# Unit spacing, four accumulator banks at the end, earlier value copies and a split last tile in an attention + feed-forward kernel

## Chip, cores, metric

The kernel runs on one core of a Trainium2 chip. The metric is device time in microseconds (us).

The engines: PE is TensorE (matmuls), PEld its weight loads, DVE VectorE, ACT ScalarE, POOL GpSimd, SP SyncE.

## Reference

```python
# q, k, v: (8 batches, 8 heads, 576, 64); bias_table: (32, 8)
scores = q @ k.T / 8 + bias(bucket(|i - j|), head)
x = softmax(scores) @ v            # as (4608 tokens, 512)
out = ((x @ w_a) * (x @ w_b)) @ w_out      # w_a, w_b: (512, 1536), w_out: (1536, 512)
```

Inputs and output are float32, and the kernel computes with bfloat16 operands.

## The kernel before

Attention goes through 32 slots, one for each batch and pair of heads. A slot makes scores on PE (`qk`), their exponentials on ACT (`ex`, 128x1024 each), scales these by a bias factor on DVE (`mul`), and multiplies the previous slot's weights by the values (`av`). The feed-forward network of a finished batch fills PE in between, as *units*. A unit is four 512-column matmuls into one PSUM bank: `pa` (emptied by ACT into `ha`), `pb` (emptied by DVE, multiplied by `ha`, into `g`), or a third of an output tile `po`. There are 9 chunks of 512 tokens, 36 units each (the first chunk has 44, some of them half as wide). The last two chunks run after attention has ended.

```python
# PSUM, 8 banks: scores 2 x 2 banks, av 1, transposes 1, feed-forward 2
ps_sc = pool(bufs=2); ps_av = pool(bufs=1); ps_tr = pool(bufs=1); ps_ff = pool(bufs=2)
wrk = pool(bufs=2)                 # SBUF: ha, output tiles ob, reciprocals: two of each
# ... cut ...
def ff_b(c, df, lo=0, n=512):
    pb = ps_ff.tile([128, 512], FP32, tag="ffn")
    for mc in range(4):
        nc.tensor.matmul(out=pb[:, 0:n], lhsT=wb_sb[df // 4][:, mc, ...], rhs=xn_sb[mc][...], ...)
    nc.vector.tensor_tensor(out=g_sb[df][...], in0=pb[...], in1=ff["ha"][...], op=MULT)
# ... cut: ff_a is the same with w_a, and an ACT copy to ha ...
def ff_o(c, tt, part):             # token tile tt, a third of 12 matmuls
    ...
    if part == 2:
        ob = wrk.tile([128, DM], FP32, tag="ob")
        nc.scalar.activation(out=ob, in_=po, func=Copy)
        # last chunk: two stores of 64 rows, both issued by ACT
        for hh in range(2):
            nc.scalar.dma_start(out=out[r0:r0 + ST, :], in_=ob[64 * hh:64 * hh + 64, :])
# ... cut ...
# one slot s; U puts a unit, A(...) are the previous slot's values
steps = [(qk(s, 0), ex(s, 0)),
         U, ex(s, 1), A(0, 1, 2), U, mul(s, 0), t_q(s + 1), U,
         mul(s, 1), A(3, 4), (qk(s, 2), ex(s, 2)), U,
         ex(s, 3), t_k(s + 1), U, t_x(s - 1), mul(s, 2), U, mul(s, 3), U,
         (qk_tail(s), ex_tail(s)), U, U, mul_tail(s)]
# ... at the end of every slot:
v_next(s)                          # even slots: DVE copies the values of four heads into vm
```

Between the second score pair `qk(s, 2)` and `qk_tail` stand four units in a row with nothing else on PE.

The softmax here doesn't subtract the row's maximum and nothing guards it: scores larger than these inputs give would overflow.

## Time and profile before

Three runs: 431.69 us median (430.83 to 432.91).

| read from the trace of before | value |
|---|---|
| PE busy | 412.0 of 430.5 us |
| spacing of 512-column matmuls | 0.216 us |
| a pair pa + pb, last two chunks | 1.875 us (eight matmuls: 1.72) |
| a DVE product `g` from a bank | 0.69 us |
| value copy on DVE | 0.42 us |
| ACT copy of 128x512 from PSUM | 0.60 us |

From the page of the kernel before come the busy times (us, share of the span, instructions; one line) and the chain that ended last:

```profile
PE 412.0 (96%) x3406; PEld 210.3 (49%) x3459; DVE 238.0 (55%) x560; ACT 248.1 (58%) x346; POOL 130.0 (30%) x187
...
PE 88%; DVE 7%; issue 2%; ACT 1%; DVEq 0%; ACTq 0%
```

PE sets the time. But 96% busy does not mean 4% of holes. A matmul's record lasts 0.38 us while the next can start 0.216 us after it, so records overlap and cover small holes. Holes are read from the starts. A few matmul records are missing, and a gap of exactly one more matmul (0.216 us) is such a record.

The timeline of before in the last chunk (start, duration, engine, line, what; in brackets idle time and what ended it):

```profile
397.15 0.38 PE L492 MATMUL pa_2_0_5469<-xn_134,wa_124 128*128 128x512 bf16 x1
...
397.51 0.38 PE L502 MATMUL pb_2_0_5476<-xn_131,wb_127 128*128 128x512 bf16 x1
...
398.65 0.69 DVE L505 TENSOR_TENSOR g_137<-pb_2_0_5476,ha_2_0_5474 128x512 bf16<-128x512 f32 x1 [1.18 <-PE pb_2_0_5476 L502]
...
399.02 0.38 PE L492 MATMUL pa_3_0_5482<-xn_134,wa_124 128*128 128x512 bf16 x1
...
399.39 0.38 PE L502 MATMUL pb_3_0_5489<-xn_131,wb_127 128*128 128x512 bf16 x1
```

The last matmul of pa starts at 397.15 and the first of pb at 397.51: 0.36 us instead of 0.216. At 398.65 DVE begins to empty that pb's bank and ends at 399.34. The next pb starts at 399.39, while the matmul before it started at 399.02. Every pair loses 0.15 us to a bank that is not yet empty.

The timeline of before, PE only, in slot 17, after its second score pair:

```profile
185.08 0.38 PE L330 MATMUL qk_3_2905<-QB_116,KB_118 64*128 64x512 bf16 x2
185.39 0.39 PE L502 MATMUL pb_1_0_2910<-xn_131,wb_127 128*128 128x512 bf16 x1
...
186.26 0.38 PE L492 MATMUL pa_2_0_2918<-xn_131,wa_124 128*128 128x512 bf16 x1
...
186.91 0.38 PE L492 MATMUL pa_2_0_2918<-xn_134,wa_124 128*128 128x512 bf16 x1
187.28 0.38 PE L502 MATMUL pb_2_0_2928<-xn_131,wb_127 128*128 128x512 bf16 x1
...
189.00 0.22 PE L384 MATMUL qkt_2942<-ZB_120,KB_118 128*128 128x128 bf16 x1
```

From 186.91 to 187.28 is 0.37 us: the same hole. It opens at the third unit of the row, the pb at 187.28: DVE's product from the row's first bank, pb(1), ran from 186.53 to 187.22 (the same timeline, DVE only):

```profile
186.53 0.69 DVE L505 TENSOR_TENSOR g_136<-pb_1_0_2910,ha_1_0_2875 128x512 bf16<-128x512 f32 x1 [0.31 <-PE pb_1_0_2910 L502]
```

The timeline of before at the start of slot 19, with the value copy:

```profile
203.89 0.42 DVE L318 COPY vm_101<-vn_97 128x1024 bf16<-128x1024 bf16 x1
204.01 0.22 PE L448 MATMUL av_0_3153<-vt_103,att_113 128*128 128x130 bf16 x1
...
204.36 0.19 PE L452 MATMUL av_0_3153<-vm_101,at_0_2976 128*128 128x65 bf16 x1
```

The value matmul that reads `vm` (line 452) starts 0.35 us after the one ahead of it, just when the copy (203.89 to 204.31) has ended.

The timeline of before at the end (ACTq is ACT's sequencer issuing two stores):

```profile
423.22 0.60 ACT L516 ACTIVATE ob_2_5646<-po_2_5633 128x512 f32<-128x512 f32 x1 [1.99 <-PE po_2_5633 L512]
...
423.85 1.12 ACTq L523 DMA_DIRECT2D out_dram<-ob_2_5646  x2
...
425.39 0.38 PE L512 MATMUL po_3_5650<-wo,g_146 128*128 128x512 bf16 x1
425.81 0.60 ACT L516 ACTIVATE ob_3_5663<-po_3_5650 128x512 f32<-128x512 f32 x1 [1.99 <-PE po_3_5650 L512]
426.44 1.12 ACTq L523 DMA_DIRECT2D out_dram<-ob_3_5663  x2
```

### The profile page before, as it was taken

How to read it: one execution, taken by the hardware profiler on the slowest of the kernel's cores; microseconds unless marked ns; L12 is line 12 of the kernel's file. 1: busy time of each engine (PE TensorE's matmuls, PEld its weight loads, DVE VectorE, ACT ScalarE, POOL GpSimd, SP SyncE). 2: the span in 40 equal slices, each digit the busy share in tenths (PEclk: the TensorE clock that was granted, in tenths of full speed). 3: DMA queues.
4: the chain of work that ended last, by engine and by line, in shares of the span. 5: the costliest groups of instructions: out<-in, count | busy, mean ns of one | idle time of the engine just before them, and what ended most of it. 6: DMA issues, size and time to landing. Idle time of an engine off the chain costs nothing.

```text
span 430.5 us, 8709 instructions
## 1 busy us (share of the span) xinstructions
PE 412.0 (96%) x3406; PEld 210.3 (49%) x3459; DVE 238.0 (55%) x560; ACT 248.1 (58%) x346; POOL 130.0 (30%) x187
## 2 busy tenths in 40 slices
PE   8689899999999999999999999999999999999995
PEld 3366545455455545554555545544555454344442
DVE  5789667566654665466646664666546642321320
ACT  4676676676656666676566665676566642323221
POOL 9655458694009500870069004200000000000000
PEclk9789999999999999999999999999999999999999
DMA  8999999999149924995399919960420011002004
GB/s 110 195 202 186 205 138 186 163 175 152 23 88 162 160 36 87 132 146 77 63 118 145 120 24 123 123 88 14 109 56 15 15 40 73 1 24 75 0 2 98
DMA packets 139596, 42.46 MB, mean 99 GB/s; under 512 B 115962, under 2 KB 134938, under 8 KB 139554
## 3 DMA queue, kind: packets, MB, share of 16 engines
q0 software_dynamic: 81264, 18.89, 55.2%
q1 hardware_dynamic: 52850, 13.54, 21.7%
q10 hardware_dynamic: 5440, 9.47, 7.1%
q8 instruction: 27, 0.44, 0.5%
q14 instruction: 15, 0.12, 0.1%
HBM read 39.18 MB, written 9.45 MB: 113 GB/s over the span
## 4 chain that ended last, share of the span: by engine, by line
PE 88%; DVE 7%; issue 2%; ACT 1%; DVEq 0%; ACTq 0%
PE warm L207 1%; DVE g_143 L505 1%; PE trb L268 1%; DVE att_113 L419 1%; PE po_2_4609 L512 1%; PE po_2_3999 L512 1%; PE po_2_3376 L512 1%; PE po_2_2753 L512 1%; PE po_2_2130 L512 1%; PE po_1_2670 L512 1%; PE po_1_3916 L512 1%; PE po_3_5650 L512 1%; PE po_0_5379 L512 1%; PE po_0_5084 L512 1%; PE po_0_3878 L512 1%
## 5 line engine op out<-in xcount | busy, mean ns | idle before, releaser
L492 PEld LDWEIGHTS <-wa_124 128*128 128x128 bf16 x160 | 14.7, 98 | 17.8 <-issue 3.9
L502 PEld LDWEIGHTS <-wb_128 128*128 128x128 bf16 x144 | 13.3, 97 | 20.3 <-issue 7.1
L159 POOL DMA_DIRECT2D vt_104<-in_v_dram x8 | 4.9, 626 | 58.9 <-PE av_3_2722 L452 27.7
L502 PEld LDWEIGHTS <-wb_129 128*128 128x128 bf16 x144 | 12.9, 97 | 18.8 <-issue 7.0
L502 PEld LDWEIGHTS <-wb_127 128*128 128x128 bf16 x160 | 14.1, 97 | 16.2 <-issue 5.9
L159 POOL DMA_DIRECT2D vt_103<-in_v_dram x8 | 5.1, 645 | 55.5 <-PE av_3_3345 L452 27.4
L492 PEld LDWEIGHTS <-wa_125 128*128 128x128 bf16 x144 | 12.9, 98 | 16.5 <-issue 2.9
L492 PEld LDWEIGHTS <-wa_126 128*128 128x128 bf16 x144 | 12.9, 98 | 16.2 <-issue 2.8
L130 POOL DMA_DIRECT2D qn_93<-in_q_dram x24 | 18.3, 818 | 6.9 <-DMA wo<-in_moe_w_out_dram 6.1
L139 POOL DMA_DIRECT2D kn_95<-in_k_dram x24 | 18.2, 801 | 5.0 <-PE pb_3_256_951 L502 2.7
L130 POOL DMA_DIRECT2D qn_94<-in_q_dram x24 | 18.2, 807 | 2.2 <-DMA vn_97<-in_v_dram 1.9
L139 POOL DMA_DIRECT2D kn_96<-in_k_dram x24 | 18.1, 795 | 0.2 <-PE pb_11_0_1307 L502 0.2
L419 DVE TENSOR_TENSOR att_113<-att_113,W_88 128x512 bf16<-128x512 bf16 x8 | 3.4, 426 | 14.2 <-ACT att_113 L409 14.2
L448 PEld LDWEIGHTS <-att_114 128*128 128x128 bf16 x76 | 7.5, 99 | 3.9 <-DVE XG_123 L462 0.7
L408 ACT ACTIVATE att_114<-trb 128x64 bf16<-128x64 f32 x14 | 3.1, 224 | 10.8 <-PE trb L392 10.8
L408 ACT ACTIVATE att_113<-trb 128x64 bf16<-128x64 f32 x14 | 3.1, 224 | 10.7 <-PE trb L392 10.7
L448 PEld LDWEIGHTS <-att_113 128*128 128x128 bf16 x76 | 7.4, 98 | 3.6 <-DVE att_113 L421 0.2
L419 DVE TENSOR_TENSOR att_114<-att_114,W_91 128x512 bf16<-128x512 bf16 x8 | 3.4, 427 | 7.6 <-ACT att_114 L409 7.6
L505 DVE TENSOR_TENSOR g_135<-pb_0_0_5450,ha_0_0_5448 128x512 bf16<-128x512 f32 x1 | 0.7, 693 | 11.4 <-PE pb_0_0_5450 L502 11.4
L512 PEld LDWEIGHTS <-g_135 128*128 128x128 bf16 x36 | 3.5, 97 | 7.0 <-issue 4.5
L207 PE MATMUL warm<-zero_sb 128*128 128x512 bf16 x11 | 5.2, 581 | 1.5 <-DVE zero_sb L199 1.2
L121 POOL DMA_DIRECT2D vn_97<-in_v_dram x8 | 6.6, 828 | 0.0
(2743 smaller groups left out, 1515.9 us busy)
## 6 DMA issues: line engine op xcount, KB each, us to landing
vn_97<-in_v_dram POOLq DMA_DIRECT2D x8, 256.0 KB, 6.3
vn_98<-in_v_dram POOLq DMA_DIRECT2D x8, 256.0 KB, 7.0
wo<-in_moe_w_out_dram POOLq DMA_DIRECT2D x1, 1536.0 KB, 16.2
kn_95<-in_k_dram POOLq DMA_DIRECT2D x24, 64.0 KB, 5.2
qn_93<-in_q_dram POOLq DMA_DIRECT2D x24, 64.0 KB, 4.7
kn_96<-in_k_dram POOLq DMA_DIRECT2D x24, 64.0 KB, 4.9
qn_94<-in_q_dram POOLq DMA_DIRECT2D x24, 64.0 KB, 4.0
qn_93<-in_q_dram POOLq DMA_DIRECT2D x4, 128.0 KB, 4.2
```

The source lines that it names most:

```text
L121: nc.gpsimd.dma_start(out=dst[:, 256 * h0:256 * h1].rearrange("p (h x) -> p h x", x=256), in_=src[b, h0:h1, 0:SM, :].rearrange("h (p t) d ...
L130: nc.gpsimd.dma_start(out=by_tile(qn[b % 2])[:, h0 // 4, t, :, :], in_=q[b, h0:h1, 128 * t:128 * t + 128, :].transpose([1, 0, 2]))
L139: nc.gpsimd.dma_start(out=by_tile(kn[b % 2])[:, h0 // 4, t, :, :], in_=k[b, h0:h1, t:SM:NM, :].transpose([1, 0, 2]))
L159: nc.gpsimd.dma_start(out=vt[b % 2][64 * hh:64 * hh + 64, :, hh, 0:Dh], in_=v[b, hh:H:2, SM:S, :].transpose([1, 0, 2]))
L207: nc.tensor.matmul(out=warm[:, :], lhsT=zero_sb[:, 0:128], rhs=zero_sb[:, :], start=True, stop=True)
L408: nc.scalar.activation(out=at[:, m:m + ST], in_=pt, func=ACTF.Exp, scale=scale)
L419: nc.vector.tensor_tensor(out=x, in0=x, in1=e, op=MULT)
L448: nc.tensor.matmul(out=pav[:, slot, :, :], lhsT=weights_tail(p, jq), rhs=vt[i][:, hp, :, :], start=True, stop=True)
L492: nc.tensor.matmul(out=pa[:, 0:n], lhsT=wa_sb[df // 4][:, mc, 128 * (df % 4):128 * (df % 4) + 128], rhs=xn_sb[mc][:, 512 * c + lo:512 * c ...
L502: nc.tensor.matmul(out=pb[:, 0:n], lhsT=wb_sb[df // 4][:, mc, 128 * (df % 4):128 * (df % 4) + 128], rhs=xn_sb[mc][:, 512 * c + lo:512 * c ...
L505: nc.vector.tensor_tensor(out=g_sb[df][:, lo:lo + n], in0=pb[:, 0:n], in1=ff["ha"][:, 0:n], op=MULT)
L512: nc.tensor.matmul(out=po[:, :], lhsT=g_sb[df][:, 128 * tt:128 * tt + 128], rhs=wo_sb[:, df, :], start=(df == 0), stop=(df == NDF - 1))
```

## The change

Four ideas: (1) never more than two units in a row, with the late values or scores in between; (2) in the last two chunks, when no scores are made any more, units take turns on four banks, two of them from the score pool; (3) the value copy is made in mid-slot, a whole half slot before it is needed; (4) the last token tile is made in two column halves, each copied by ACT and DVE together and stored by SP and ACT in parallel.

```diff
+    def ff_bank(name):
+        ff["n"] += 1
+        if ff["late"] and ff["n"] % 4 >= 2:
+            return ps_sc.tile([128, 2, 512], FP32, tag="sc", name=name)[:, 0, :]
+        return ps_ff.tile([128, 512], FP32, tag="ffn", name=name)
 # pa, pb and po come from ff_bank (cut)
+    def ff_o_last(c, tt, half):
+        cs = slice(256 * half, 256 * half + 256)
+        po = ff_bank(f"po{c}_{tt}_{half}")
+        for df in range(NDF):
+            nc.tensor.matmul(out=po[:, 0:256], lhsT=g_sb[df][:, 128 * tt:128 * tt + 128],
+                             rhs=wo_sb[:, df, cs], start=(df == 0), stop=(df == NDF - 1))
+        ob = wrk.tile([128, DM], FP32, tag="ob", name=f"ob{c}_{tt}_{half}")
+        nc.scalar.activation(out=ob[:, 0:128], in_=po[:, 0:128], func=ACTF.Copy)
+        nc.vector.tensor_copy(out=ob[:, 128:256], in_=po[:, 128:256])
+        for hh, eng in enumerate((nc.sync, nc.scalar)):
+            r0 = S * (2 * tt + hh) + SM
+            eng.dma_start(out=out[r0:r0 + ST, cs], in_=ob[64 * hh:64 * hh + 64, 0:256])
 # ... cut ...
-            steps += [U, lambda: ex(s, 1), A(0, 1, 2), U, lambda: mul(s, 0), lambda: t_q(s + 1), U,
-                      lambda: mul(s, 1), A(3, 4), lambda: (qk(s, 2), ex(s, 2)), U,
-                      lambda: ex(s, 3), lambda: t_k(s + 1, ACT), U, lambda: t_x(s - 1),
-                      lambda: mul(s, 2), U, lambda: mul(s, 3), U,
-                      lambda: (qk_tail(s), ex_tail(s)), U, U, lambda: mul_tail(s)]
+            head = [U, lambda: ex(s, 1), A(0, 1, 2), U, lambda: mul(s, 0), lambda: t_q(s + 1), U,
+                    lambda: mul(s, 1)]
+            late = [A(3, 4), U, lambda: t_x(s - 1)]
+            pair = [lambda: v_next(s), lambda: (qk(s, 2), ex(s, 2)), U, lambda: ex(s, 3),
+                    lambda: t_k(s + 1, ACT), U, lambda: mul(s, 2)]
+            tail = [lambda: (qk_tail(s), ex_tail(s)), U, U, lambda: mul_tail(s)]
+            if s % 4 == 0:
+                steps += head + late + [U] + pair + [lambda: mul(s, 3)] + tail
+            else:
+                steps += head + pair + late + [lambda: mul(s, 3), U] + tail
         else:
+            ff["late"] = True
 # ... cut ...
-        if new:
+        if s == 4:
             v_next(s)
```

More of the change, by code (lines that the diff above doesn't have):

```diff
@@ L484, in t_x @@
             copy(eng, xn_sb[hp][:, c0:c0 + ST], ps[:, SM - q0:S - q0])
-    ff = {}
+    ff = {"late": False, "n": 0}
+    def ff_bank(name):
[3 more added lines that the diff above has]
+        return ps_ff.tile([128, 512], FP32, tag="ffn", name=name)
     def ff_a(c, df, lo=0, n=512):
-        pa = ps_ff.tile([128, 512], FP32, tag="ffn", name=f"pa{c}_{df}_{lo}")
+        pa = ff_bank(f"pa{c}_{df}_{lo}")
         for mc in range(NMC):
@@ L499, in ff_b @@
     def ff_b(c, df, lo=0, n=512):
-        pb = ps_ff.tile([128, 512], FP32, tag="ffn", name=f"pb{c}_{df}_{lo}")
+        pb = ff_bank(f"pb{c}_{df}_{lo}")
         for mc in range(NMC):
@@ L505, in ff_b @@
         nc.vector.tensor_tensor(out=g_sb[df][:, lo:lo + n], in0=pb[:, 0:n], in1=ff["ha"][:, 0:n], op=MULT)
+    def ff_o_last(c, tt, half):
[10 more added lines that the diff above has]
+            eng.dma_start(out=out[r0:r0 + ST, cs], in_=ob[64 * hh:64 * hh + 64, 0:256])
     def ff_o(c, tt, part):
         if part == 0:
-            ff["po"] = ps_ff.tile([128, 512], FP32, tag="ffn", name=f"po{c}_{tt}")
+            ff["po"] = ff_bank(f"po{c}_{tt}")
         po = ff["po"]
@@ L536 @@
         for tt in range(4):
+            if c == NCH - 1 and tt == 3:
+                units += [lambda c=c, tt=tt, half=half: ff_o_last(c, tt, half) for half in range(2)]
+                continue
             for part in range(3):
```

## The prediction

> **What bounds it.** TensorE. The page has PE busy 412.0 of 430.5 us (96%), DVE 55%, ACT 58%; the chain of waits is 88% PE. Busy hides waiting here, because a matmul record (0.38 us) is longer than the spacing of matmuls. So I read the spacing of starts in the timeline: 512-column matmuls start every 0.216 us (the Trainium skill, "TensorE: Matmul & The Clock Gate", Back-to-back issue gap, gives N/2.4 + 2.5 ns, also 216: the trace agrees), a feed-forward unit of 4 takes 0.86 us, a pair 1.72 us. Gaps of exactly one matmul are missing records. Granted clock is 1.00 after 30 us. The diff removes no matmul work; only holes in this stream can be saved.
>
> **Holes it aims at:**
>
> 1. Last two chunks (360 to 418 us): only two feed-forward banks. A pair takes 1.875 us, as at 397.51, 399.39, 401.26: pb starts right after DVE has emptied the preceding pb (0.69 us, starting 0.4 us after its matmuls). 22 holes of 0.15 us, 3.3 us in all. With four banks in rotation (two from the idle score pool) DVE (0.69 per 1.72 us) and ACT (0.60) keep up. Saved: 3.1 us.
> 2. Same hole from 75 to 346 us: four units stand in a row after the second score pair. 18 holes of 0.153 us, 2.75 us. With at most two in a row, 0.5 us or more of other matmuls lies in between, so a bank has 1.36 us to drain instead of 0.86; some 1.1 are needed. Working the order through with traced durations, exponentials (1.02 us) and scalings (0.68) leave only 0.1 us of slack in slots where DVE also has the value copy. Saved: 2.3 us.
> 3. Value copies (0.42 us on DVE) end a slot; the next slot's first value matmul waits for them: 0.30 us at 113.5, 158.8, 204.0, 249.3 and 340.1 us, 0.65 at 294.5. The one at 49.8 us (0.42) stays, since slot 4 keeps its order. Saved: 2.1 us.
> 4. Tail. Now: last matmul starts 425.39, ACT copy 425.81 to 426.41, two stores issued in turn by ACT (426.44, 426.95), last landing about 429.4, then 1.1 us of ending. The change shortens the copy to about 0.25 us and issues the stores in parallel: 0.9 us less on paper. But there are only two output buffers: the second half takes the third token tile's, whose second store is issued at 424.35 and lands at 426.76. So both last copies, ready near 425.9, wait until 426.8; stores issue near 427.1 and land near 429.2 (2.0 to 2.4 us from issue in this trace). ACT and DVE reading one bank may also be serialised. Saved: 0.2 us.
>
> Sum 7.7 us, less some 0.3 for new small waits: 7.4, all on the critical path, since PE is it.
>
> **Prediction:** 431.7 - 7.4 = 424.3 us, 8 in 10 between 422.4 and 427.5. Faster by over 2%: 0.14; within 2%: 0.85; slower: 0.01.
>
> **Right if:** pairs in the last two chunks are 1.72 us; the 0.153 us gaps before pb nearly vanish from 75 to 346 us; the first value matmul no longer waits for vm; PE busy stays at 405 to 412 us while the span shrinks. In the tail, the last ACT and DVE copies show idle ended by the store of ob_2.
>
> **Wrong if:** earlier second scores wait for the first exponentials' banks, or the moved work delays DVE so that new holes open before qk or pb (gain 4 to 5 us); four banks still wait for ACT; the 256-column matmuls are held up by their 24 weight loads (0.1 us each); or the stores land sooner (0.7 us more).

## More of the kernel before

`t_x(s - 1)` issues, on SP, two transposing DMAs that bring the normalized result into `xn_sb`, which the feed-forward units read.

## The result

425.47 us median of 4 runs (425.10 to 425.94), against 432.19 (430.83 to 432.91, 4 runs) of the kernel before. The ratio is 0.9839, 95% interval 0.9815 to 0.9863. Ratios here and below are the mean time of one kernel's fast runs over that of the other's of the same rounds, so not quite the ratio of the medians quoted. The change saves 6.7 us by the medians; 7.4 were forecast, and the time lies in the forecast range (422.4 to 427.5).

The page after:

```profile
PE 407.6 (96%) x3471; PEld 207.6 (49%) x3471; DVE 239.0 (56%) x562; ACT 245.6 (58%) x347; POOL 130.7 (31%) x187
...
PE 85%; DMA 7%; POOL 3%; DVE 2%; ACT 1%; issue 1%; ACTq 0%; DVEq 0%; POOLq 0%
```

PE busy fell by 4.4 us while the span fell by 6.9, with no matmul work removed: matmul records had also covered waiting.

The timeline after, PE only, in the last chunk, where equal matmuls are merged with their count:

```profile
389.10 1.03 PE L498 MATMUL pa<-xn,wa 128*128 128x512 bf16 x4
389.96 1.03 PE L508 MATMUL pb<-xn,wb 128*128 128x512 bf16 x4
390.83 1.03 PE L498 MATMUL pa<-xn,wa 128*128 128x512 bf16 x4
391.69 1.03 PE L508 MATMUL pb<-xn,wb 128*128 128x512 bf16 x4
```

Units start every 0.86 to 0.87 us, and a pair takes 1.73 us. No hole is left in these pairs.

The timeline after, PE only, slot 17 again:

```profile
184.23 0.38 PE L330 MATMUL qk<-QB,KB 64*128 64x512 bf16 x2
184.54 1.04 PE L508 MATMUL pb<-xn,wb 128*128 128x512 bf16 x4
185.42 1.03 PE L498 MATMUL pa<-xn,wa 128*128 128x512 bf16 x4
186.28 0.22 PE L448 MATMUL av<-vt,att 128*128 128x130 bf16 x1
...
186.65 0.42 PE L452 MATMUL av<-vm,att 128*128 128x65 bf16 x8
186.91 1.02 PE L508 MATMUL pb<-xn,wb 128*128 128x512 bf16 x4
187.77 1.03 PE L498 MATMUL pa<-xn,wa 128*128 128x512 bf16 x4
188.64 0.39 PE L384 MATMUL qkt<-ZB,KB 128*128 128x128 bf16 x4
```

Two units, then values (A(3, 4)), then two units, and then the tail of the scores. All starts follow each other by the time that their columns take.

The timeline after, with the value copy of slot 18 and the first values of slot 19:

```profile
196.52 0.42 DVE L318 COPY vm<-vn 128x1024 bf16<-128x1024 bf16 x1
...
203.50 0.22 PE L448 MATMUL av<-vt,att 128*128 128x130 bf16 x1
...
203.56 0.42 PE L452 MATMUL av<-vm,at 128*128 128x65 bf16 x8
```

The copy is now made 7 us before the matmul that reads it, and this one starts 0.06 us after the one ahead of it.

The timeline after, at the end:

```profile
415.65 2.71 PEld L517 LDWEIGHTS <-g 128*128 128x128 bf16 x24
415.87 2.78 PE L517 MATMUL po<-wo,g 128*128 128x256 bf16 x24
...
416.69 1.12 ACTq L542 DMA_DIRECT2D out_dram<-ob  x2
417.94 0.28 ACT L520 ACTIVATE ob<-po 128x128 f32<-128x128 f32 x1 [1.27 <-PE po L517]
418.25 0.29 DVE L521 COPY ob<-po 128x128 f32<-128x128 f32 x1 [9.19 <-ACT ob L520]
418.57 2.26 SPq L524 DMA_DIRECT2D out_dram<-ob  x2
418.57 0.50 ACTq L524 DMA_DIRECT2D out_dram<-ob  x1
419.70 0.28 ACT L520 ACTIVATE ob<-po 128x128 f32<-128x128 f32 x1 [1.49 <-DMA out_dram<-ob]
420.01 0.29 DVE L521 COPY ob<-po 128x128 f32<-128x128 f32 x1 [1.47 <-ACT ob L520]
420.34 0.50 ACTq L524 DMA_DIRECT2D out_dram<-ob  x1
```

Two things stand here that the change did not intend. The last ACT copy (419.70) waited 1.49 us for a store of the third token tile to land (issued at 417.20, landed at 419.60), because it reuses that tile's buffer. And DVE starts each of its copies 0.03 us after ACT has ended its own: they take turns. No run tells whether they do so for the PSUM bank that both read or for the output tile that both write. ACT alone needs 0.60 us for 512 columns, and the two in turn 0.28 + 0.03 + 0.29 us for 256.

There is one new wait of more than 0.25 us, in the first unit of the second chunk in slot 9 (the timeline after, PE only):

```profile
90.05 0.82 PE L498 MATMUL pa<-xn,wa 128*128 128x512 bf16 x3
91.77 0.38 PE L498 MATMUL pa<-xn,wa 128*128 128x512 bf16 x1 [0.89 <-DMA kn<-in_k_dram]
```

The fourth matmul of this `pa` reads the part of `xn` that the last transpose of the batch brings. The releaser named there is a load; the experiments below name the transpose.

Stages, worked out from the starts of ACT and DVE records, of which none is missing (112 exponentials of 128x1024, 112 products in each trace). A slot runs from its first 128x1024 exponential on ACT to that of the next; a chunk's units from its first DVE product (of 512 columns) to its last; the end from the third token tile's ACT copy to the span's end. Two stretches that took the same in both, 12.09 us between the products of the last two chunks and 7.70 us from the last product to the third tile's copy, are left out of the rows but are in the sum. All are us from one trace each:

| stage | before | after | difference |
|---|---|---|---|
| slots 8 and 9 | 19.96 | 21.02 | +1.06 |
| slots 10 to 30 | 237.72 | 233.79 | -3.93 |
| slot 31 to the first product of the next to last chunk | 22.66 | 22.22 | -0.44 |
| products of the next to last chunk | 20.97 | 18.99 | -1.98 |
| products of the last chunk | 20.66 | 18.99 | -1.67 |
| third token tile's copy to the end | 7.24 | 7.54 | +0.30 |
| start of slot 10 to the end, all | 329.04 | 321.32 | -7.72 |

### The profile page after: what moved, and what is told of

The parts are those of the page before. It is cut to its first block, busy times and chain, and to the rows that moved or that the text cites. A ratio compares the mean times of both kernels' runs of the same rounds, so it can differ in the third digit from the quotient of the medians.

```text
span 423.6 us, 8798 instructions
## 1 busy us (share of the span) xinstructions
PE 407.6 (96%) x3471; PEld 207.6 (49%) x3471; DVE 239.0 (56%) x562; ACT 245.6 (58%) x347; POOL 130.7 (31%) x187
## 4 chain that ended last, share of the span: by engine, by line
PE 85%; DMA 7%; POOL 3%; DVE 2%; ACT 1%; issue 1%; ACTq 0%; DVEq 0%; POOLq 0%
PE pb L508 22%; PE pa L498 22%; PE po L531 21%; PE av L452 9%; PE qk L330 7%; DMA kn<-in_k_dram 4%; PE av L448 2%; DMA wb<-in_moe_w_b_dram 2%; PE qkt L384 1%; PE qkt L388 1%; POOL qn L121 1%; POOL vt L159 1%; POOL kn L121 1%; POOL tl L153 1%; DMA out_dram<-ob 1%
## 5 line engine op out<-in xcount | busy, mean ns | idle before, releaser
L337 ACT ACTIVATE at<-qk 128x1024 bf16<-128x1024 f32 x112 | 111.5, 1024 | 29.1 <-PE qk L330 11.1
L511 DVE TENSOR_TENSOR g<-pb,ha 128x512 bf16<-128x512 f32 (+1 forms) x112 | 75.1, 671 | 79.4 <-PE pb L508 61.5
L498 PE MATMUL pa<-xn,wa 128*128 128x512 bf16 (+1 forms) x448 | 112.1, 372 | 1.8 <-DMA kn<-in_k_dram 0.9
L508 PE MATMUL pb<-xn,wb 128*128 128x512 bf16 (+1 forms) x448 | 111.8, 372 | 0.1
L502 ACT ACTIVATE ha<-pa 128x512 f32<-128x512 f32 (+1 forms) x112 | 65.2, 582 | 73.5 <-PE pa L498 73.5
L531 PE MATMUL po<-wo,g 128*128 128x512 bf16 x420 | 99.1, 379 | 0.0
L342 DVE TENSOR_TENSOR at<-at,W 128x1024 bf16<-128x1024 bf16 x112 | 75.0, 684 | 20.5 <-ACT at L337 20.5
L498 PEld LDWEIGHTS <-wa 128*128 128x128 bf16 x448 | 40.2, 98 | 48.0 <-issue 8.3
L508 PEld LDWEIGHTS <-wb 128*128 128x128 bf16 x448 | 39.6, 98 | 46.3 <-issue 9.7
L452 PE MATMUL av<-vm,at 128*128 128x65 bf16 x896 | 41.2, 194 | 0.2 <-DVE vm L318 0.2
```

The costliest lines, as they stand in the source:

```text
L337: nc.scalar.activation(out=at[:, :, :], in_=ps[:, :, :], func=ACTF.Exp, scale=scale)
L342: nc.vector.tensor_tensor(out=at[:, :, :], in0=at[:, :, :], in1=w[:, :, S - 1 + t:S - 1 + t - SM:-1], op=MULT)
L452: nc.tensor.matmul(out=pav[:, slot, hh, :], lhsT=weights(p, t, hh, jq), rhs=vm[i][:, 2 * hp + hh, t, :], start=False, stop=True, skip_grou ...
L498: nc.tensor.matmul(out=pa[:, 0:n], lhsT=wa_sb[df // 4][:, mc, 128 * (df % 4):128 * (df % 4) + 128], rhs=xn_sb[mc][:, 512 * c + lo:512 * c ...
L502: nc.scalar.activation(out=ha[:, 0:n], in_=pa[:, 0:n], func=ACTF.Copy)
L511: nc.vector.tensor_tensor(out=g_sb[df][:, lo:lo + n], in0=pb[:, 0:n], in1=ff["ha"][:, 0:n], op=MULT)
```

## The experiments

All kernels gave correct results. Each was timed for five rounds, on one chip with the kernel before for each set of four.

**Theory:** four independent savings that add up, but for the end, where the split tile costs a little. **Rivals:** the middle's two parts are redundant; the split end helps as meant; the new wait in slot 9 is the price of the new order.

### One part of the change alone: set 1

*only_banks*: the kernel before with `ff_bank` and `ff["late"]`.

> Kernel before, with the score banks lent to the last two chunks and nothing else. My theory: the two feed-forward banks alone make the 0.15 us holes after 360 us, so in the trace the stretch from the first to the last DVE product of the last two chunks shortens by 3.2 to 3.6 us, nothing moves before it, and the time falls by 3.3 us, 0.8% (ratio 0.992). Rival: the last two chunks wait for DVE or ACT as such and not for a bank, or the gain needs the other order too: then the stretch shortens by less than 1 us.

Measured: 428.29 us against 432.60 (ratio 0.9896, 0.9866 to 0.9927). Products of the last two chunks took 18.99 and 18.99 us instead of 20.97 and 20.66, and slots 10 to 30 took 237.77, as before. So two banks were the limit there and four remove it, by 3.65 us. DVE and ACT keep up.

*only_order*: the kernel before with the new step lists, without `v_next` in `pair`.

```diff
-            pair = [lambda: v_next(s), lambda: (qk(s, 2), ex(s, 2)), U, ...
+            pair = [lambda: (qk(s, 2), ex(s, 2)), U, ...
```

> Kernel before, with at most two feed-forward units in a row, value copies left at the end of the slot, no lent banks, no split tail. My theory: 0.15 us is won in three of four slots from slot 10 on, about 2.7 us by slot 31, the 0.3 us waits of the first value matmul for the copy stay, and about 0.9 us is lost again before slot 10, because the transposes of slot 7 are issued later. Net minus 1.8 us, ratio 0.996. Rival: the loss at slot 10 in the changed kernel belongs to the moved copy or to chance; then there is no loss here, and net minus 2.7 us.

Measured: 431.98 us (429.97 to 433.26), ratio 0.9976, 0.9940 to 1.0013. The stages bear out the first half: three of four slots are 0.15 us shorter, slots 10 to 30 take 235.37 us (-2.35), the stage after them 22.51 (-0.15), and the waits for `vm` remain. But slots 8 and 9 took 24.82 us, 4.9 more than in the trace of before. The timeline of *only_order*, PE only:

```profile
88.58 0.82 PE L492 MATMUL pa<-xn,wa 128*128 128x512 bf16 x3
92.41 0.38 PE L492 MATMUL pa<-xn,wa 128*128 128x512 bf16 x1 [3.01 <-DMA xn<-XG]
```

The transposed values are now named as the releaser. The profile also shows when a DMA landed. This last transpose was issued at 83.91 us and landed 8.46 us later; in before it was issued at 85.57 and landed after 4.62 us. Both were issued 4.1 us after the start of slot 8, so the transpose that is waited for is not issued later in the new order. That the wait is large here does not show that the order causes it, because the next two kernels have the old order there and wait too.

*only_vcopy*: the kernel before, with the copy ahead of the second score pair.

```diff
-  lambda: mul(s, 1), A(3, 4), lambda: (qk(s, 2), ex(s, 2)), U,
+  lambda: mul(s, 1), A(3, 4), lambda: v_next(s), lambda: (qk(s, 2), ex(s, 2)), U,
```

> Kernel before, with only the value copies moved ahead of the second score pair. My theory: the six waits for the copy after slot 8 go (0.3 us each, one 0.65) and the time falls by about 2.1 us, ratio 0.995; slot 10 loses nothing. Rival: DVE is then late elsewhere (copy before the products in four units in a row) and the waits only move: gain under 1 us.

Measured: 430.34 us, ratio 0.9945, 0.9913 to 0.9977. Slots 10 to 30 are 1.81 us shorter and the stage after them 0.29: together 2.10 us, as said. Slots 8 and 9 took 21.96.

*only_tail*: the kernel before with `ff_o_last`, on the two feed-forward banks.

> Kernel before, with only the last token tile in two halves. My theory: nothing is won: 24 matmuls of 256 columns take 0.13 us more than 12 of 512, ACT and DVE copy one after the other, 0.6 us as before, and both wait for the store of the third tile; the trace is 0.1 to 0.4 us longer from the copy of the third token tile to the end, ratio 1.000 to 1.001. Rival: the intent holds and the end comes 0.5 to 0.9 us sooner.

Measured: 431.92 us, ratio 0.9983, 0.9954 to 1.0011. From the third tile's copy to the end its trace took 7.79 us against 7.24, so the trace was 0.55 us longer there, more than the 0.1 to 0.4 expected; the timed rounds do not resolve this. The end is a stage that differs between traces by 0.1 us with a whole tile and by 0.3 us with this split (see *no_tail*). The last ACT copy again sat idle until a store had landed, here for 1.76 us. Slots 8 and 9: 21.09 us, with code equal to before in all the stages up to there.

What follows from the stages of set 1: the parts add. From slot 10 up to the third tile's copy, 2.50 (order) + 2.10 (copies) + 3.65 (banks) = 8.25 us, and the whole change saves 8.02 us there. The missing 0.23 us lie in slot 14, where the kernel after has a hole of 0.24 us before a pb that none of the single parts has. It is in every trace that has order and copy together with the units placed alike. DVE's product of the unit after the copy starts 0.35 us later there than in slot 18, which has the same steps; what holds that unit back is not settled.

### The slot-9 wait and the end: set 2

*after_again*: the changed kernel once more.

> The changed kernel once more, as a yardstick on this chip. Both theories: ratio 0.984 give or take 0.003; every slot from 10 to 30 as in its first trace within 0.02 us (but for one odd gap of 0.24 us in slot 14), last two chunks 18.99 us each between their first and last product. My theory: slot 9 differs from trace to trace (0 to 1.5 us and more over 10.80), because the first unit of the second chunk waits for the last transpose of the first batch's values, which shares the queues with loads. Rival: the 0.9 us there is a fixed cost of this change, and slot 9 is 11.7 us again within 0.1.

Measured: 426.19 us (425.04 to 427.86) against 432.14, ratio 0.9858, 0.9836 to 0.9881. The stages from slot 10 on repeat (321.31 against 321.32 us). Slot 9 took 12.16 us instead of 11.71, so this stage does differ from one execution to the next.

*no_tail*: the changed kernel with the last token tile whole (the three lines that put `ff_o_last` removed).

> The changed kernel with the last token tile whole again. My theory: the split tail costs 0.3 us, so from the copy of the third token tile to the end 7.24 us as in the kernel before, against 7.54; the ratio is that of the changed kernel or 0.001 below. Rival: halves and parallel stores do help once the rest of the change is there: the end comes 0.3 us or more later without them.

Measured: 424.00 us, ratio 0.9819, 0.9795 to 0.9843. From the third tile's copy to the end 7.24 us, against 7.53 in *after_again*. Over all traces, this stage took 7.24 to 7.35 us with the whole tile (*before*, *only_order*, *no_tail*, *only_banks*, *only_vcopy*), and 7.53 to 7.85 us with the split on the shared buffer (*after*, *after_again*, *shift*, *only_tail*, *defer*). So the split costs 0.3 us or somewhat more, and never gained. The two longest ends, *only_tail* and *defer*, are those where the last ACT copy sat idle longest, 1.76 and 1.80 us, until a store had landed. The rest of the difference in time to *after_again* is not from the end: slots 8 and 9 took 19.97 us here and 21.48 there.

*tail_own_one*: own buffers for the halves, each copied by one engine.

```diff
-        ob = wrk.tile([128, DM], FP32, tag="ob", ...)
-        nc.scalar.activation(out=ob[:, 0:128], in_=po[:, 0:128], func=ACTF.Copy)
-        nc.vector.tensor_copy(out=ob[:, 128:256], in_=po[:, 128:256])
+        ob = wrk.tile([128, 256], FP32, tag="ol", ...)
+        copy(nc.scalar if half == 0 else nc.vector, ob[:, 0:256], po[:, 0:256])
```

> The changed kernel, where the two halves have two output buffers of their own and each is copied by one engine (ACT the first, DVE the second). My theory: the last copy then waits for no store, starts some 0.4 us after the last matmul instead of 1.3, takes 0.35 to 0.45 us instead of twice 0.28 in turn, and the stores land 2.1 us after issue: from last matmul to end 4.1 to 4.3 us instead of 5.23, ratio 0.002 to 0.003 below the changed kernel. Rival: the end is set by how long stores take, not by the buffer, and less than 0.4 us is won.

Measured: 424.13 us, ratio 0.9801, 0.9779 to 0.9823. From the last matmul's start to the end 4.08 us against 5.23. The timeline of *tail_own_one* at the end:

```profile
417.21 0.38 ACT L258 ACTIVATE ol<-po 128x256 f32<-128x256 f32 x1 [1.20 <-PE po L517]
417.62 1.43 SPq L523 DMA_DIRECT2D out_dram<-ol  x2
417.62 1.36 ACTq L523 DMA_DIRECT2D out_dram<-ol  x2
418.03 0.42 DVE L260 COPY ol<-po 128x256 f32<-128x256 f32 x1 [9.63 <-PE po L517]
```

The DVE copy of the second half (418.03) is released by the matmuls and not by a store. Now the split pays: 6.39 us from the third tile's copy, 0.85 less than the whole tile of before.

*defer*: in every fourth slot, the transposes of the next batch's second half are issued after `t_x`.

```diff
-        if s % 4 == 0 and 2 <= b - 1 < B:
-            t_half(b - 1, 1)
-                steps += head + late + [U] + pair + ...
+                steps += head + late + [lambda: t_half(b - 1, 1), U] + pair + ...
```

> The changed kernel, where in every fourth slot the transposes of the next batch's second half are issued after the last transpose of the batch's values, not ahead of it. My theory: the wait of the second chunk's first unit is queueing behind those transposes; slot 9 falls to 10.7 to 11.0 us in its trace, the spread of the times narrows, and the mean falls by 0.5 to 1.5 us, ratio 0.001 to 0.004 below the changed kernel. Rival: the wait comes from the loads' traffic alone: slot 9 stays between 11 and 13 us and the time does not move.

Measured: 424.52 us (424.08 to 425.22), ratio 0.9818, 0.9795 to 0.9840. Slots 8 and 9 took 20.81 us and the wait was still 0.7 us. The ratio is 0.004 below *after_again*, but the two intervals overlap, and *no_tail*, which leaves those transposes where they are, moved by as much. So queueing behind those transposes is not shown to be the cause, and not excluded as a part of it.

### Which part of the end, and a later second chunk: set 3

*tail_own*: own buffers (`tag="ol"`), both engines still copying each half.

> The changed kernel with own output buffers for the two halves, each half still copied by ACT and DVE. My theory: two causes share the 1.15 us that own buffers with one copy engine won at the end: the buffer 0.9, the two copies in turn 0.2 to 0.3. So from last matmul to end 4.2 to 4.4 us, against 5.23 in the changed kernel and 4.08 with one copy engine. Rival: taking turns is all of it, and the end stays above 4.8 us; or it costs nothing, and the end is 4.1 us.

Measured: 424.72 us (423.61 to 427.43), ratio 0.9833, 0.9801 to 0.9865. From last matmul to end 4.55 us. The buffer is worth 0.68 us (5.23 to 4.55) and one copy instead of two in turn, with all that follows, 0.47 (4.55 to 4.08): the second was undersized in what I expected. Each figure is from single traces. And the 0.47 is not all turn-taking, as the timeline of *tail_own* shows:

```profile
421.23 0.50 ACTq L524 DMA_DIRECT2D out_dram<-ol  x1
421.77 0.28 ACT L520 ACTIVATE ol<-po 128x128 f32<-128x128 f32 x1 [0.90 <-PE po L517]
```

The last ACT copy starts 0.66 us after the last matmul (421.11), just when ACT's queue has issued the first half's store. In *tail_own_one* the last copy is on DVE and starts 0.31 us after the last matmul. So 0.35 us is an earlier start, and 0.18 us the shorter copy (0.42 instead of 0.60). That the store's issue held ACT's copy back fits the times, but no run tests it alone. The time is poor for another reason: slots 8 and 9 took 24.65 us in this trace.

*shift*: one unit fewer in slot 8.

```diff
-    quotas = {4: 12, 5: 8, 6: 7, 7: 7, 8: 6}
+    quotas = {4: 12, 5: 8, 6: 7, 7: 7, 8: 5}
```

> The changed kernel with one feed-forward unit fewer in slot 8, so that the second chunk starts one unit later, behind the first values of slot 9. My theory: its first unit then starts some 2.1 us later and waits 0 to 0.5 us for the transposed values where the six traces of the changed order so far had 0 to 5 us; 0.5 to 1 us is won on average, ratio 0.001 to 0.003 below the changed kernel, if the other pairing of units opens no new holes. Rival: the transposes come that much later too, since they follow the same slot, and nothing is won; or new holes of 0.15 us or more in every slot eat it.

Measured: 424.56 us (423.25 to 425.31), ratio 0.9813, 0.9790 to 0.9836. Slots 8 and 9 took 19.79 us, with 0.17 us of waiting for the transposed values; but this kernel does one unit less in them, and the stage after slot 30 is 0.70 us longer for it. In slot 8 there is a new wait of 0.62 us, where the scores of the tail (`qk_tail`) wait for an exponential on ACT (it stands in *best* and *best_defer* too). Slots 10 to 30 took 233.89 us against 233.79. So moving the unit keeps most of the wait for the transpose away, and costs 0.62 us in slot 8 and 0.1 us later. That the time falls is not shown: the intervals of *shift* and *after_again*, from two sets, just touch, and that of the first rounds (0.9815 to 0.9863) overlaps with both.

*best*: *tail_own_one* and *shift* together.

> The changed kernel with own output buffers and one copy engine for each half, and the second chunk one unit later. My theory: both gains add: from last matmul to end 4.1 us, ratio 0.978 to 0.981 against the kernel before, faster than the changed kernel by 1.5 to 2.5 us. Rival: no better than own buffers alone (0.980).

Measured: 422.58 us (422.19 to 423.59), ratio 0.9781, 0.9758 to 0.9803; 4.00 us from last matmul to end.

*best_defer*: *best* and *defer* together.

> The kernel labelled best, with the half-batch transposes of every fourth slot also issued behind the last value transpose. My theory: with the second chunk already later, nothing is left to win: ratio within 0.001 of best. Rival: another 0.5 us or more, if queueing behind those transposes still counts.

Measured: 422.35 us (421.55 to 422.48, 4 runs), ratio 0.9762, 0.9740 to 0.9784. Its interval and that of *best* overlap widely, so it isn't shown to be better than *best*. Against the kernel before it is faster by 2.4%, which the change as given (1.4 to 1.6%) is not.

### The wait of slots 8 and 9 over the traces

The last transpose's time from issue to landing, and slots 8 and 9, for the traces with the unit count of before in slot 8 (*defer*, where the profile has no landing for it, is left out):

| kernel | issued at, us | landed after, us | slots 8 and 9, us |
|---|---|---|---|
| before | 85.57 | 4.62 | 19.96 |
| no_tail | 85.20 | 5.27 | 19.97 |
| tail_own_one | 85.37 | 5.69 | 20.39 |
| only_banks | 83.78 | 6.12 | 20.94 |
| only_tail | 83.58 | 6.25 | 21.09 |
| after | 85.39 | 6.33 | 21.02 |
| after_again | 84.59 | 6.79 | 21.48 |
| only_vcopy | 84.59 | 7.15 | 21.96 |
| tail_own | 84.49 | 8.29 | 24.65 |
| only_order | 83.91 | 8.46 | 24.82 |

Up to small differences, the longer it takes to land, the longer the stage, for old and new order alike. With either order the stage takes 19.96 or 19.97 us where PE does not wait (before and *no_tail*). In each of the other eight traces, the fourth matmul of the unit starts 0.03 to 0.05 us after this transpose has landed. So the transpose is what PE waits for, also where the profile names a load.

In this stage the one trace of before was a lucky one: *only_banks* and *only_tail*, with the same code there, took 1.0 and 1.1 us more. So the 1.06 us of the first two traces do not show a cost of the change. But they do not show that there is none. The code up to slot 4 is the same in all kernels, and yet slot 4 starts at 35.66 to 37.69 us. The trace of before started it last and had no wait, while *only_banks* and *only_tail* started it first of these ten. Counted from the span's start to slot 10, before took 101.42 us, *only_banks* 100.61 and *only_tail* 100.54; the six traces of the table with the new order took 101.05 to 105.01, and *only_vcopy*, old order and earlier copies, 102.45. A cost of the new order before slot 10 is thus not excluded. Whether it makes long waits more frequent (both stages of over 24 us were with it) stays open; so does why the landing takes between 4.6 and 8.5 us. All these traces have loads by POOL under way at that time.

## Why the prediction was right, and where it was off

- **Bound by PE, only holes to save: right.** PE busy 407.6 us after (405 to 412 were said), no work removed.
- **Holes of the last two chunks: right in mechanism, a little small.** 3.1 us were forecast and 3.65 measured (*only_banks*). Most of the surplus is one hole that the count of 0.15 us each had missed, 0.50 us before `pb_6` at 372.26 us in before. There the DVE product that empties the bank started 0.84 us after its last matmul instead of 0.4; why is not settled.
- **Four units in a row: right.** 2.3 forecast; 2.50 in *only_order*, of which 0.24 goes again in slot 14 when the copy is in mid-slot too.
- **Value copies: right.** 2.1 forecast, 2.10 in *only_vcopy*.
- **Tail: the right wait, the wrong sign.** The step that failed is "Saved: 0.2 us", and in it "stores issue near 427.1". The wait for the third tile's buffer came as said: the last copies were to start 3.6 us after the third tile's copy (423.22 to 426.8), and the last ACT copy started 3.63 us after it (416.07 to 419.70). But from there to the stores' issue 0.3 us were reckoned, with a copy of about 0.25 us and turn-taking as a mere possibility. The two copies took turns, 0.60 us, and the last store was issued 0.64 us after the start of the first. That is most of the miss; about 0.1 us more lies in the landing. The half-width matmuls are not part of it: 24 of them at 0.109 us take 0.03 us more than 12 at 0.216, and they were done about 1 us before the store let the copy start. The measured term is +0.30 us in the first pair of traces, 0.2 to 0.6 between any two traces of the two kinds.
- **New small waits, 0.3 us: the size fits slot 14 (0.24), by luck.** The allowance named no place. The wait for transposed values was not foreseen. It is there with the old order too (*only_banks*, *only_tail*, *only_vcopy*) and differs between executions.
- **The sum.** From slot 10 to the end the trace gained 7.72 us, against 7.4 forecast for the whole. It is so close in part because misses cancel: banks and order won 0.55 and 0.2 us more than forecast, the tail 0.5 us less. The timed gain was 6.7 us by the medians of the first rounds and 6.0 in *after_again*. The rest lies before slot 10 (0.87 us more in the trace after than in that of before), where the start and slots 8 and 9 differ between executions by 2 us and more. One trace for each kernel does not average that, and how much of it is the change's stays open.

## What to carry to other kernels

When the bounding engine's records overlap, count holes from the starts of instructions and not from busy time, and size each part of a change from its own holes: such parts add, as three of four did here within 0.25 us. Before splitting a last tile to shorten the end, look at which buffer the last piece will take and when that one's store lands; and two engines that copy halves of one bank into one tile did not halve the copy here. When one trace has a new wait, look for it in several traces of kernels with the same code there before putting it down to the change.

## What the Trainium skill lacked or had wrong

- "TensorE: Matmul & The Clock Gate", Back-to-back issue gap, gives about 131 ns per matmul for a sustained stream of weight load and matmul pairs at 512 columns. These traces show 0.216 us with a weight load for every matmul: eight of them in 1.73 us (the timeline after, last chunk). The page's isolated gap, N/2.4 + 2.5 ns, is what holds here. At 256 columns too: the 24 matmuls at the end of the timeline after take 2.78 us, of which the last record is 0.27, so they start every 0.109 us, as that formula gives.
- "PSUM — Partial Sum Buffer", PSUM bank collisions raise a hardware error, says that two engines must not read the same bank and quadrant at once. The trace agrees with its consequence, DVE starting 0.03 us after ACT in each half. No run separates the bank from the output tile as the reason. The page lacks what that costs: 256 columns split between ACT and DVE took 0.60 us, as much as 512 columns on ACT alone (0.60), while one engine took 0.38 (ACT) or 0.42 us (DVE) for the 256.
- "DMA: Bandwidth & Descriptors", DMA Transpose (X-bar), has no figure for how long a transposing DMA takes to land while loads are under way. Here it was 4.6 to 8.5 us from issue for one and the same transpose, and it set the time of a stage.
